# Transposed maxima on SP's queue, the projected values' rooms by turns, and another order for the first attention block

## The chip, the cores and the metric

The kernel runs on one core of a Trainium2 chip. The metric is the device time of one execution in microseconds, the median of several runs. The profiled execution has a time of its own, given below beside its span.

## The reference

Two attention blocks A and B are computed from inputs of their own, both with S = 2048 tokens, D = 512, H = 32 heads of 16 channels, in f32. A is a sliding window of 256 tokens, B sees all tokens.

```python
qkv = (x @ wqkv).reshape(B, S, 3, H, Dh)            # -> q, k, v: B, H, S, Dh
scores = einsum("bhqd,bhkd->bhqk", q, k) * Dh ** -0.5
# A only: mask = (i - j >= 0) & (i - j < 256), others to -1e9
p = softmax(scores, axis=-1)
o = einsum("bhqk,bhkd->bhqd", p, v)
out = o.transpose(...).reshape(B, S, D) @ wo
return concatenate([a, b], axis=-1)                 # 1, 2048, 1024
```

## The kernel before

**Precision.** PE's products are f32 or a split f32. An input is split into a rounded part and a rest (`split`, L137 on ACT and L138 on DVE or POOL), and a product of two split tiles is three matmuls (`products`, L183). One projection of 128 by 512 is so 4 x 3 = 12 matmuls.

**Projections.** There are 96 of them, 48 for each block, named in ORDER_P: `Aq20` is block A, queries, pair 2 of head groups, chunk 0 of 512 tokens, and `Av13` is block A, values, chunk 1, token tile 3 of that chunk. Queries and keys (`project_qk`) are evacuated by ACT (L241 or L245), split again on DVE (L251) or POOL (L255, L256), and stored to DRAM as `parts` (L263). From there they come back as `opk` (keys, `load_k_now`, L293) and `oq` (queries, `load_q_now`, L309), in a layout with 16 rows for each part of a head. Values (`project_v`) are evacuated by ACT into one of two SBUF rooms `vst` (L321) and stored as `vd` (L329); they return as `vt` (L337).

**Attention.** For each unit (block, head group of four heads, chunk of 512 queries) the largest score of each query is found first (`max_item`: matmuls at L416 for A and L368 for B, DVE at L421, L425, L426 or L372). `max_finish` negates the maxima and splits them in three bf16 parts, `max_rows` transposes them on PE (L464), ACT copies them to `ntr` (L466), and two transfers at L471 put them as three further rows under the queries in `oq`. With three rows of ones under the keys, the score matmul (`scores`, L497) so subtracts the maximum itself. ACT takes the exponential (L504), POOL masks A's tiles (L514), and `weigh` (L543, A) or `weigh2` (L528, B) multiplies with the values and a column of ones. The result goes to DRAM (`od`, L561), is normalised on POOL (L615 to L618), and projected by `wo`.

**Order.** All is scheduled by hand at build time. The block before B's attention runs by two strings. ORDER_A has a letter for each item on PE: `p` a whole projection (the next of ORDER_P), `m` a maximum, `t` a transposition of maxima, `s` a score step, `w` a weighing step, `e` an early maximum of B. The loop takes the letters strictly in turn. Products `p` and `t` use all rows of PE's array, `m`, `s` and `e` halves of it by rows, `w` quarters of it by columns. Around them a `Model` of the engines runs at build time; it decides where in the program the loads and the deferred work of the other engines are put: a load is written out when the model's time for PE has reached the time at which its data and room are there. Each engine then carries out its own instructions in the order written. The second block (B's attention) follows a fixed pattern and is not touched by ORDER_A.

**Transfers.** All are issued by SP, but for the rows of A's maxima (L471), which ACT issues. Each transfer signals one of eight semaphores, given out in turn over both queues, so that a transfer waits at its issue for the one eight places earlier to have landed. The model before has no such semaphores, and counts A's rows at L471 as ACT's time.

Of the kernel before, what the change touches and what calls it, by code (L numbers as in the profile page):

```python
# [11 lines left out]
F32 = mybir.dt.float32  # L12
# [18 lines left out]
KS = 3 * DH  # L31
KM = KS + 3
ROW = 0, 64
# [11 lines left out]


ORDER_P = (
# [4 lines left out]
    "Bq20 Bk13 Bk31 Bk30 Bq10 Bq30 Bk33 Bq31 Bq33 Bq32 Bk21 Bk32 ").split()  # L52
FIRST = 4.0
FINAL = 34.5
LOADS = 4.0
# [3 lines left out]


ORDER_A = (
    "ppppppppppmmpmmpmmpmmpmmptmmpmmpmsmpmsmpmsmpsmmtpmmswsmpswmmsptwmmspsmwmsmpsmwsmmpmswsmpsmmwtsmptmms"
    "psmmpmswsmpmswmsmpmswsmmswsmmswtmsmpsmmwsmsmwsmmstwmsmpsmwsmtwmmspmmswsmmswsmpsmmswsmmwsmsmtmspmmwsm"
    "psmmwsmtwsmmpmsmtmswmswsmsmmswmspmswmmswmspmssmwtsmmpmswtmsmpsmwsmswmssmmwsmpmmpmmswsmmswtsmmpsmmwsm"
    "smwstmmwsmpmsmwswsmmpmssmwtmsmpmssmmtwsmmpmswmsmsmwmssmtwsmmsmwmsmswmspsmwsmmswtmsmpwsmmswsmmpmswsmm"
    "psmmswtmsmpmswmsmpmmswtmsmpsmwmsmpsmwtmmspmswsmpsmwsmpmswtsmmpsmwsmwmspmswsmwtmmspswmmspsmmpsmwtmsmp"
    "smwmsmpmsmwspmsmwsmtwsmmpsmmwsmpsmwmsmpmswmsmpsemtwsmpemtpmsmwsmpmswemspsemswsempsempmswmmspmsmwsmtw"
    "mmspsempsmmwwtmsmpesmpmswsmmpsemswsmmswtmsmpmswmsmpesmwsmwmswemspsempemswwemtpesmpsmmwsmpemspmmswsmp"
    "mmtpsmmpmmwwm")
LAND = 700  # L70
LAND_V = 2000
LGAP = 2500
# [4 lines left out]
class Model:  # L77
# [4 lines left out]
    def __init__(self):  # L82
        self.t = {e: 0 for e in ("PE", "ACT", "DVE", "Pool", "SP", "DMA")}
        self.mode, self.turn = "f", 170
        self.banks = {"e": [0] * 3, "p": [0] * 2, "o": [0]}

    def run(self, engine, ns, *after):
        self.t[engine] = max(self.t[engine], *after, 0) + ns
# [6 lines left out]
        return self.run("PE", turn + ns, *after)  # L95

    def dma(self, kb, *after):
        t = self.run("SP", 450, *after) + 600
        self.t["DMA"] = max(self.t["DMA"], t) + int(4.0 * kb)
        return self.t["DMA"] + 1300  # L100

    def bank(self, pool, n=0):

# [15 lines left out]
def attention_kernel(ctx: ExitStack, tc: tile.TileContext, xT, wqk, wv, wo, out):  # L119

    nc = tc.nc
# [7 lines left out]
    M = Model()  # L129
    ready = {}  # L130
    obank = [None]
    ns = 0
    xs, ws, parts, vd, opq, mt, pts, pvt, od, rl, osp = {}, {}, {}, {}, {}, {}, {}, {}, {}, {}, {}
# [74 lines left out]
    vst = [cst.tile([128, H, VW], F32, name=f"vst{i}") for i in range(2)]  # L208
# [72 lines left out]
    def load_ones(g):  # L281
        for a in range(2):
            nc.sync.dma_start(opk2(g)[ROW[a] + KS:ROW[a] + KM].bitcast(F32), one_d.rearrange("(s r) t -> s r t", s=3))
            ready["ones", g % 2] = M.dma(48, ready["ones"])

    def load_k_now(b, g, c0, c1, t):

        ops = opk2(g)
        for a in range(2):
            for r, n in ((0, 2), (2, 1)):  # L290
                for c in range(c0, c1):
                    tok = slice(c * QC, c * QC + QC)
                    nc.sync.dma_start(ops[ROW[a] + 16 * r:ROW[a] + 16 * (r + n), :, tok].bitcast(F32),  # L293
                                      heads_of(b, g, 1, a)[0:n, :, :, tok])
                    t1 = M.dma(64 * n, t)
        for c in range(c0, c1):
            ready["k", b, g, c] = t1

# [4 lines left out]
    def load_q_now(b, g, c, t):  # L303

        oq = sb.tile([128, HG // 2, QC], F32R, name=f"oq_{b}_{g}_{c}", tag="oq", bufs=4)
        opq[b, g, c] = oq
        for a in range(2):
            for r, n in ((0, 1), (1, 2)):
                nc.sync.dma_start(oq[ROW[a] + 16 * r:ROW[a] + 16 * (r + n)].bitcast(F32),  # L309
                                  heads_of(b, g, 0, a)[0:n, :, :, c * QC:(c + 1) * QC])  # L310
                t1 = M.dma(64 * n, t)
        ready["qd", b, g, c] = t1

    def project_v(b, c, a):

        kt = 4 * c + a
        bank, ps = room()
        yield from products(ps, [(lambda u, i=i: xs[b, c, i][:, u, 128 * a:128 * a + 128], lambda v, i=i: ws[b, "v", i][:, v])
                      for i in range(4)])
        v = vst[kt % 2]  # L320
        nc.scalar.activation(v[:, :, 0:DH], ps.rearrange("p (h d) -> p h d", d=DH), AF.Copy)  # L321
        t = M.run("ACT", 480, M.t["PE"] + WAKE)
        release(bank, t)
        ready["vd", b, kt] = M.dma(272, t)
        slots_v.pop(0)
        slots_v.append(ready["vd", b, kt])
        if b not in vd:
            vd[b] = dram.tile([NG // 2, S, VP], F32, name=f"vd_{b}")
        nc.sync.dma_start(vd[b][:, kt * 128:kt * 128 + 128].rearrange("p t n -> t p n"),  # L329
                          v.rearrange("p (g h) d -> p g (h d)", g=NG // 2))  # L330
# [5 lines left out]
    def load_v_now(b, p, k0, k1, t):  # L336
        nc.sync.dma_start(vt[p % 2][:, k0:k1, 0:VP],  # L337
                          vd[b][p, k0 * 128:k1 * 128].rearrange("(k t) n -> t k n", t=128))
        t = M.dma(68 * (k1 - k0), t)
        for kt in range(k0, k1):  # L340
            ready["v", b, p, kt] = t

# [46 lines left out]
    def load_early_k(c):  # L389
        gap[0] = M.t["PE"] + GAP  # L390
        for a in range(2):
            for r, n in ((0, 2), (2, 1)):
                nc.sync.dma_start(ke()[ROW[a] + 16 * r:ROW[a] + 16 * (r + n), c * QC:c * QC + QC].bitcast(F32),
                                  heads_of(1, 0, 1, a)[0:n, :, 0, c * QC:c * QC + QC])
                ready["ke", c] = M.dma(32 * n)

    def max_item(b, g, c, qt, j, kc):
        n = f"{b}_{g}_{c}_{qt}_{j}_{kc}"
# [60 lines left out]
    def max_rows(b, g, c):  # L459
        n = f"{b}_{g}_{c}"  # L460
        nm = parts["nm"]
        bank, ps = room()
        ps = ps.bitcast(BF16)
        nc.tensor.transpose(ps[:48, :128], nm.rearrange("p a s j q -> p (a s j q)"), ident)  # L464
        nt = sb.tile([48, 128], F32, name=f"ntr_{n}", tag="ntr")
        nc.scalar.activation(nt, ps[:48, :128], AF.Copy)  # L466
        t = M.run("ACT", 200, M.pe("f", 60, ready["nm", b, g, c]))
        release(bank, t)
        for a in range(2):
            ready["q", b, g, c] = M.dma(12, t) if b else M.run("ACT", 775) + 2300  # L470
            (nc.sync if b else nc.scalar).dma_start(opq[b, g, c][ROW[a] + KS:ROW[a] + KM].bitcast(F32).rearrange(  # L471
                "s r (q t) -> s (r q) t", t=128), nt[24 * a:24 * a + 24])


# [280 lines left out]
    def pair(b, p):  # L755
        return [(project_qk, b, p, 1 - s, c) for c in range(NQC) for s in range(2)]

    def values(b):
        return [(project_v, b, c, a) for c in range(NQC) for a in range(4)]
# [16 lines left out]
    got = lambda its: all(x in made for x in its)  # L776
# [25 lines left out]
    def later_load(it, cond, f, *a):  # L802

        u = place.get(it, 0) - LOADS
        def g(*a):
            lgap[0] = M.t["PE"] + LGAP
            f(*a)
        list_("load", lambda: pos() >= u and cond(), lambda: max(lgap[0], free("stage")()), g, *a)
# [4 lines left out]
    for b, p in groups:  # L813
        its = values(b) if p == "v" else [] if p == "o" else pair(b, p)
        for s in range(4 if p in ("v", "o") else 2):
            before = slots_of[len(slots_of) - 8] if len(slots_of) >= 8 else []
            slots_of.append(its)
            cond = lambda before=before: got(before)
            it = its[0] if its else bursts[-1][1]
            later_load(it, cond, *((load_wv, b, s) if p == "v" else (load_wo, b, s) if p == "o" else  # L820
                                   (load_wqk, b, p, 1 - s)))
        if (b, p) == (1, 0):
            for c in range(NQC):
                for i in range(4):
                    later_load(pair(1, 0)[2 * c], lambda c=c: got(pair(0, 3)[0:2 * c + 2]), load_x, 1, c, i)

    def stored(b, p, s, cs):
        return lambda: max(ready.get(("parts", b, p, s, c), NEVER) for c in cs)
# [57 lines left out]
    while todo_a or gen[0]:  # L886
# [8 lines left out]
        i, j = divmod(ns, HG)  # L895
        t = NEVER
        if gen[0]:
            t = pe
        elif x == "p":
            t = max(bank(), operands(bursts[nb][1]))  # L900
        elif x == "t" and nts:
            t = max(ready["nm", *nts[0]], bank())
        elif x == "w" and k < i:
            un, (m, pieces), a, z = flat[k]
            t = max(*(ready.get(("v", 0, un[1] // 2, y[0]), NEVER) for y in pieces), ready["p", *un, m],
                    M.bank("o") if a else 0)
# [178 lines left out]
```

## Time and profile before

| | |
|---|---|
| median of 3 runs | 1906.01 us (1904.59 to 1915.66) |
| profiled execution | 1913.99 us, span 1912.3 us, granted clock 0.982 |
| PE busy | 1858.8 us (97%) |
| DVE busy | 1540.0 us (81%) |
| ACT busy | 1407.3 us (74%) |
| POOL busy | 469.2 us (25%) |
| instructions | 37273 |
| transferred | 166.68 MB |

Times in the profile count from the start of the span. PE is TensorE, PEld its weight loads, DVE VectorE, ACT ScalarE, POOL GpSimd, SP SyncE; a `q` behind an engine's name is its sequencer, which issues transfers. `L497` is line 497 of the program. A group of instructions is written as line, engine, operation, output<-inputs. A row of waits names who waited, for whom, how long in total, how many times, and the longest. Matmuls overlap, and their ends are modelled.

### The profile page before, as it was taken

Reading aid. Unit: us, or ns where it says so; the run is one execution under the profiler, and the core shown is the slowest. Engines: PE = TensorE matmul, PEld = TensorE weight load, DVE = VectorE, ACT = ScalarE, POOL = GpSimd, SP = SyncE. Lnnn points to the kernel's source line nnn. Section 1 sums busy time; section 2 is a strip of 40 time slices with the busy share of each in tenths; the row PEclk is TensorE's granted clock in tenths of the full one; section 3 lists DMA queues with packets and bytes.
Section 4 is the critical chain, followed back from the end, with each engine's and each line's share of the span. In section 5 each row is a group of like instructions: output and inputs, shape, how many; then the busy total and the mean of one; then the engine's idle time right before and its main releaser. Section 6 shows DMA issues by size and latency. Waiting matters only on the chain.

```text
span 1912.3 us, 37273 instructions
## 1 busy us (share of the span) xinstructions
PE 1858.8 (97%) x14376; PEld 935.9 (49%) x14376; DVE 1540.0 (81%) x2320; ACT 1407.3 (74%) x2754; POOL 469.2 (25%) x896
## 2 busy tenths in 40 slices
PE   7999898899999999999999999999999999999999
PEld 6665565566655455544444444444444444444436
DVE  4557578556657967699999999999999999999910
ACT  4256566555545867688888888888888888898883
POOL 0167677635564422001100000010001000001010
PEclk9999899899988999999999999999999999999999
DMA  7655565555445223411120031120031121010002
GB/s 246 178 176 166 162 181 174 172 140 161 152 142 166 82 82 90 97 41 33 28 74 15 15 72 33 44 63 16 29 71 28 32 61 35 16 37 21 30 30 94
DMA packets 129137, 166.68 MB, mean 87 GB/s; under 512 B 22996, under 2 KB 58836, under 8 KB 128948
## 3 DMA queue, kind: packets, MB, share of 16 engines
q1 hardware_dynamic: 127232, 163.52, 30.2%
q8 instruction: 113, 1.85, 0.4%
q10 hardware_dynamic: 1728, 0.79, 0.2%
q14 instruction: 64, 0.52, 0.1%
HBM read 94.49 MB, written 68.19 MB: 85 GB/s over the span
## 4 chain that ended last, share of the span: by engine, by line
PE 89%; DMA 4%; DVE 3%; ACT 2%; issue 1%; SPq 1%; ACTq 0%; POOL 0%
PE ps_all L528 28%; PE ps_all L368 19%; PE ps_all L497 18%; PE ps_all L183 17%; PE ps_all L543 4%; PE ps_all L416 2%; DVE mt L372 2%; ACT p L504 1%; DMA vd<-vst 1%; DMA in<-xT_A 1%; DMA opk<-parts 1%; PE ps_all L464 1%; DMA in<-xT_B 0%; DMA oq<-ntr 0%; DVE mt L426 0%
## 5 line engine op out<-in xcount | busy, mean ns | idle before, releaser
L504 ACT ACTIVATE p<-ps_all 128x512 f32<-128x512 f32 x2432 | 1261.6, 600 | 203.0 <-PE ps_all L497 117.7
L372 DVE TENSOR_REDUCE mt<-ps_all 128x2 f32<-128x1024 f32 x1516 | 1202.9, 869 | 89.5 <-PE ps_all L497 50.2
L497 PE MATMUL ps_all<-oq,opk 51*128 51x512 f32 (+2 forms) x2752 | 786.3, 413 | 13.9 <-ACT p L504 11.4
L368 PE MATMUL ps_all<-opk,oq 48*128 48x512 f32 x2016 | 679.2, 440 | 1.3 <-DVE mt L372 1.1
L528 PE MATMUL ps_all<-p,vt 128*32 128x256 f32 (+1 forms) x6056 | 601.5, 469 | 0.6 <-ACT ou L554 0.5
L497 PEld LDWEIGHTS ps_all<-oq,opk 51*128 51x128 f32 x2752 | 398.8, 187 | 221.1 <-ACT p L504 195.3
L368 PEld LDWEIGHTS ps_all<-opk,oq 48*128 48x128 f32 x2016 | 313.7, 185 | 321.9 <-DVE mt L372 146.5
L449 POOL TENSOR_SCALAR mm<-mm 128x16 f32<-128x16 f32 x31 | 7.8, 253 | 985.2 <-PE ps_all L497 843.3
L514 POOL TENSOR_SCALAR_AFFINE_SELECT p<-p 128x256 f32<-128x256 f32 x480 | 180.3, 407 | 234.2 <-ACT p L504 165.1
L528 PEld LDWEIGHTS ps_all<-p,vt 128*32 128x32 f32 x6056 | 119.8, 108 | 221.3 <-issue 210.6
L183 PE MATMUL ps_all<-x,w 128*128 128x512 f32 x768 | 202.5, 415 | 9.1 <-ACT w L137 9.1
L425 DVE COPY_PREDICATED ps_all<-mone,ps_all 128x256 f32<-128x256 uint16 x224 | 94.9, 424 | 119.6 <-PE ps_all L416 119.2
L183 PEld LDWEIGHTS ps_all<-x,w 128*128 128x128 f32 x768 | 146.7, 198 | 50.9 <-ACT w L137 9.3
L426 DVE TENSOR_REDUCE mt<-ps_all 128x2 f32<-128x512 f32 x224 | 155.3, 693 | 7.7
L183 PE MATMUL ps_all<-w_v,x 128*128 128x512 f32 x384 | 100.0, 412 | 5.8 <-ACT vst L321 4.4
L416 PE MATMUL ps_all<-opk,oq 48*128 48x384 f32 (+2 forms) x512 | 91.6, 378 | 11.2 <-DMA oq<-parts 9.1
L245 ACT ACTIVATE raw<-ps_all 128x512 f32<-128x512 f32 x56 | 33.4, 597 | 90.4 <-PE ps_all L183 88.1
L543 PE MATMUL ps_all<-p,vt 128*32 128x384 f32 (+2 forms) x1408 | 99.4, 398 | 0.0
L183 PE MATMUL ps_all<-w_o,x_o 128*128 128x512 f32 x384 | 90.4, 393 | 0.0
L183 PEld LDWEIGHTS ps_all<-w_v,x 128*128 128x128 f32 x384 | 72.7, 195 | 26.7 <-ACT vst L321 5.5
L183 PEld LDWEIGHTS ps_all<-w_o,x_o 128*128 128x128 f32 x384 | 71.2, 188 | 23.7 <-issue 6.7
L256 POOL TENSOR_TENSOR st<-raw,st 128x512 fp32r<-128x512 f32 x56 | 72.0, 1285 | 4.7
(58 smaller groups left out, 579.8 us busy)
## 6 DMA issues: line engine op xcount, KB each, us to landing
parts<-st SPq DMA_DIRECT2D x64, 512.0 KB
oq<-parts SPq DMA_DIRECT2D x128, 128.0 KB
opk<-parts SPq DMA_DIRECT2D x128, 128.0 KB
od<-ou SPq DMA_DIRECT2D x64, 256.0 KB
vd<-vst SPq DMA_DIRECT2D x32, 272.0 KB
oq<-parts SPq DMA_DIRECT2D x128, 64.0 KB
opk<-parts SPq DMA_DIRECT2D x128, 64.0 KB
t<-od SPq DMA_DIRECT2D x32, 256.0 KB
```

The lines of the kernel that those rows point to most:

```text
L183: nc.tensor.matmul(ps, l(u), r(v), start=start and k == 0, stop=stop and k == n - 1)
L256: nc.gpsimd.tensor_sub(two[:, 1], raw, two[:, 0].bitcast(F32))
L368: nc.tensor.matmul(ps[:, n], q[rows, 128 * qt:128 * qt + 128], k[rows, kc * QC:kc * QC + QC], start=True, stop=True)
L372: nc.vector.tensor_reduce(out=m[:, a:a + len(heads), r, qt, kc], in_=ps, axis=AX.X, op=ALU.max)
L416: nc.tensor.matmul(two[:, a, 0:w], opq[b, g, c][rows, r, 128 * qt:128 * qt + 128], opk2(g)[rows, r, t0:t1], start=True, stop=True)
L425: nc.vector.copy_predicated(two[:, :, 256:384], later, two[:, :, 0:128])
L426: nc.vector.tensor_reduce(out=m[:, :, r, qt, 0], in_=two[:, :, 128:384], axis=AX.X, op=ALU.max)
L497: nc.tensor.matmul(ps[x][:, col:col + n1], opk2(g)[rows, pr, 128 * k:128 * k + 128], opq[b, g, c][rows, pr, q0:q0 + n1], start=True, stop= ...
L504: nc.scalar.activation(p[:, a0 + x, :w], ps[x][:, :w], AF.Exp, scale=SCALE)
L514: nc.gpsimd.affine_select(out=v, in_=v, pattern=[[0, 2], [sign, 128]], compare_op=ALU.is_ge, fill=zero_fill, base=base, channel_multiplier ...
L528: nc.tensor.matmul(o[32 * j:32 * j + 32, q0:q1], vt[(g // 2) % 2][:, kt, vc:vc + 32], pts[1, g, c, kt, j // 2][:, j % 2, q0:q1], start=kt ...
L543: nc.tensor.matmul(o[32 * j:32 * j + 32, q0:q0 + w], vt[(g // 2) % 2][:, kt, vc:vc + 32], pts[b, g, c, m, j // 2][:, j % 2, col:col + w], ...
```

## The change

1. In `max_rows` the two transfers of A's rows are issued by SP, as B's already are, and no more by ACT.
2. In `project_v` the room is `vst[0]`, and the list is reversed after each use, so that the two rooms are used by turns in whatever order the values come. Before, the tile number's parity chose the room.
3. The model gives each transfer one of eight places (`lanes`) and makes SP wait for the place eight transfers back; it counts the rows of A as SP's; loads of `k`, `q`, `v` and the early ones can't start before the model's time of PE; the ones' rows are costed as 300 KB instead of 48.
4. The load of a chunk of B's input waits until all of A's projections that read the chunk before it in the same tiles are written out, not only those of pair 3.
5. ORDER_P and ORDER_A are searched anew on that model. They hold the same items in another order: 96 projections, and in ORDER_A 280 `m`, 192 `s`, 96 `p`, 96 `w`, 33 `t` and 16 `e` before and after.

```diff
 ORDER_P = (
-    "Aq00 Ak01 Ak00 Av13 Av01 Av00 Aq01 Ak02 Av22 Av03 Ak03 Aq02 Av23 Av10 Av31 Aq03 Av02 Av20 Av12 Av30 Av11 "
-    "Av21 Aq13 Ak10 Aq10 Ak20 Ak12 Av33 Ak11 Av32 Aq11 Aq12 Aq20 Ak30 Ak13 Aq31 Aq30 Aq23 Ak31 Aq22 Ak32 Bk00 "
-    "Aq21 Ak21 Ak23 Aq32 Ak22 Bq00 Aq33 Ak33 Bq02 Bk01 Bq01 Bk02 Bq03 Bk03 Bv32 Bv13 Bv00 Bv33 Bv23 Bv30 Bv11 "
...
+    "Aq00 Aq01 Ak00 Av11 Av13 Av20 Ak01 Av03 Aq02 Av01 Av22 Ak02 Av02 Av10 Aq03 Av30 Av21 Ak03 Av00 Av33 Av32 "
+    "Av12 Ak10 Aq10 Av23 Aq11 Ak20 Ak12 Av31 Aq22 Ak22 Aq13 Ak11 Aq12 Ak30 Ak13 Ak32 Ak31 Ak21 Aq30 Ak33 Aq31 "
+    "Aq20 Aq32 Aq21 Aq33 Aq23 Bk00 Ak23 Bq00 Bk01 Bk02 Bk03 Bq02 Bq03 Bq01 Bv13 Bv00 Bv02 Bv33 Bv30 Bv21 Bv32 "
...
 ORDER_A = (
-    "ppppppppppmmpmmpmmpmmpmmptmmpmmpmsmpmsmpmsmpsmmtpmmswsmpswmmsptwmmspsmwmsmpsmwsmmpmswsmpsmmwtsmptmms"
...
+    "pppppppppppmmpmmpmmpmmpmmtppmmspmmpmsmpmmspsmmtpmsmwsmsmpmsmwsmtwmspmmspmswsmmpsmwmsmpmmtpsmwsmmpmsw"
...
@@ class Model
         self.banks = {"e": [0] * 3, "p": [0] * 2, "o": [0]}
+        self.lanes = [0] * 8
...
     def dma(self, kb, *after):
-        t = self.run("SP", 450, *after) + 600
+        t = self.run("SP", 450, *after, self.lanes[0]) + 600
         self.t["DMA"] = max(self.t["DMA"], t) + int(4.0 * kb)
-        return self.t["DMA"] + 1300
+        self.lanes = [*self.lanes[1:], self.t["DMA"] + 1300]
+        return self.lanes[-1]
@@ load_ones
-            ready["ones", g % 2] = M.dma(48, ready["ones"])
+            ready["ones", g % 2] = M.dma(300, ready["ones"])
@@ load_k_now; the same for load_q_now, load_v_now, load_early_k
-                    t1 = M.dma(64 * n, t)
+                    t1 = M.dma(64 * n, t, M.t["PE"])
@@ project_v
-        v = vst[kt % 2]
+        v = vst[0]
+        vst.reverse()
@@ max_rows
-            ready["q", b, g, c] = M.dma(12, t) if b else M.run("ACT", 775) + 2300
-            (nc.sync if b else nc.scalar).dma_start(opq[b, g, c][...], nt[24 * a:24 * a + 24])
+            ready["q", b, g, c] = M.dma(12, t)
+            nc.sync.dma_start(opq[b, g, c][...], nt[24 * a:24 * a + 24])
@@ the loads of B's input
-                    later_load(pair(1, 0)[2 * c], lambda c=c: got(pair(0, 3)[0:2 * c + 2]), load_x, 1, c, i)
+                    later_load(pair(1, 0)[2 * c], lambda c=c: got([y for p in range(4) for y in pair(0, p)[0:2 * c + 2]] +
+                                                                  values(0)[0:4 * c + 4]), load_x, 1, c, i)
```

More of the change, by code (lines that the diff above doesn't have):

```diff
@@ L47 @@
 ORDER_P = (
[4 rows of a table removed]
-    "Bq20 Bk13 Bk31 Bk30 Bq10 Bq30 Bk33 Bq31 Bq33 Bq32 Bk21 Bk32 ").split()
[4 rows of a table added]
+    "Bk30 Bk31 Bq21 Bq13 Bq32 Bq23 Bk33 Bk32 Bq31 Bq33 Bk22 Bq30 ").split()
 FIRST = 4.0
@@ L61 @@
 ORDER_A = (
-    "ppppppppppmmpmmpmmpmmpmmptmmpmmpmsmpmsmpmsmpsmmtpmmswsmpswmmsptwmmspsmwmsmpsmwsmmpmswsmpsmmwtsmptmms"
[L63 to L69, printed above, removed]
+    "pppppppppppmmpmmpmmpmmpmmtppmmspmmpmsmpmmspsmmtpmsmwsmsmpmsmwsmtwmspmmspmswsmmpsmwmsmpmmtpsmwsmmpmsw"
+    "tmmspmsmwsmmswmspsmmwsmpmsmwtswmsmpmswtsmmswmspmsmswmsmpsmwtmmspsmwsmmswspmswsmpmsmwtsmmswsmpsmmwsmp"
+    "smwtsmmswsmmswsmmswmsptpwmsmswmsmswmsmsmswmsmpmwtmsmpmsmwsmmssmwmmtpmssmmwsmpsmmmwswmsmwmtpmmssmspms"
+    "mmwmswmtmswsmmsmpmmsmwtsmsmwmsmpmmssmtwsmpmsmwsmmswsmmswmsmsmptmmwsmsmwmspmmswsmpmswtmsmswmsmpmsmwts"
+    "mpsmmwsmpswmsmpsmmwsmpmsmwstwmsmpmswmmspmsmwtsmwsmmpsmwtsmmswsmpmswmsmpsmwmsmpmsmwtsmmswmspsmwtmmsps"
+    "mmswsmmswmspmswmmspmswtmsmpsmwsmmpmswsmmtpmsmwswmmspmswmsmpmswmsmptempmmswsmpemspmmswsmtwsempesmpesm"
+    "twsepemspmsmwsmwsempsmwsmmpsewsemsptempmsmwswmmspesmpmsmwsmwsmmpesmpsmmptewesmwsmwmsmpmsmpsempsmwsmm"
+    "psmmptmmwwwmm")
 LAND = 700
@@ L310, in load_q_now @@
                                   heads_of(b, g, 0, a)[0:n, :, :, c * QC:(c + 1) * QC])
-                t1 = M.dma(64 * n, t)
+                t1 = M.dma(64 * n, t, M.t["PE"])
         ready["qd", b, g, c] = t1
@@ L338, in load_v_now @@
                           vd[b][p, k0 * 128:k1 * 128].rearrange("(k t) n -> t k n", t=128))
-        t = M.dma(68 * (k1 - k0), t)
+        t = M.dma(68 * (k1 - k0), t, M.t["PE"])
         for kt in range(k0, k1):
@@ L394, in load_early_k @@
                                   heads_of(1, 0, 1, a)[0:n, :, 0, c * QC:c * QC + QC])
-                ready["ke", c] = M.dma(32 * n)
+                ready["ke", c] = M.dma(32 * n, M.t["PE"])
     def max_item(b, g, c, qt, j, kc):
@@ L469, in max_rows @@
         for a in range(2):
-            ready["q", b, g, c] = M.dma(12, t) if b else M.run("ACT", 775) + 2300
-            (nc.sync if b else nc.scalar).dma_start(opq[b, g, c][ROW[a] + KS:ROW[a] + KM].bitcast(F32).rearrange(
+            ready["q", b, g, c] = M.dma(12, t)
+            nc.sync.dma_start(opq[b, g, c][ROW[a] + KS:ROW[a] + KM].bitcast(F32).rearrange(
                 "s r (q t) -> s (r q) t", t=128), nt[24 * a:24 * a + 24])
```

2 rows, old and new, of the table ORDER_P are left out of this document.

## The prediction, made before the changed kernel was run

> **What bounds the kernel now.** I read the page first, then busy time by stretches, the waits of PE and of ACT, and last the order of time around each long wait.
>
> ```profile
> span 1912.3 us, 37273 instructions
> ```
>
> ```profile
> 0.00:603.20 603.20, 555.97 (x3908) 367.93 (x3908) 376.56 (x800) 311.19 (x615) 332.99 (x644) 0.96 0.58 172
> 603.20:1912.30 1309.10, 1302.82 (x10469) 567.98 (x10468) 1163.46 (x1521) 1096.15 (x2140) 136.24 (x252) 0.99 0.19 48
> ```
>
> ```profile
> L528 PE MATMUL ps_all<-p,vt x6056: 379/403/1061, 603.2 to 1875.2; 128*32 128x256 f32 x126, 128*32 128x512 f32 x70
> ```
>
> The columns of a stretch are PE, PEld, DVE, ACT and POOL busy, the granted clock, and DMA. L528 belongs to the second attention block alone, so the first block ends at 603.2. Behind it PE has 6.3 us of idle time in 1309; the change leaves that stage's order alone, and I put it at 0. Ahead of it PE has 603.20 - 555.97 = 47.2 us of idle time. There DVE, ACT and POOL are each under two thirds busy, so PE waits for single late events and not for a slow engine. The waits of PE in that stretch (total, times, longest):
>
> ```profile
> PE ps_all L497 <- ACT p L504: 10.9, 19, 4.4
> PE ps_all L183 <- ACT w L137: 9.1, 1, 9.1
> PE ps_all L416 <- DMA oq<-parts: 9.1, 3, 7.1
> PE ps_all L464 <- ACT raw L245: 5.2, 1, 5.2
> PE ps_all L183 <- ACT vst L321: 4.4, 1, 4.4
> PE ps_all L464 <- ACT vst L321: 2.6, 1, 2.6
> ```
>
> The 9.1 us at L183 are the first load and stay. Five of the others are single stops of 2.6 to 7.1 us, and they cost twice, because the granted clock is halved around them:
>
> ```profile
> 73.30:80.10 6.80, 5.57 (x14) 3.96 (x14) 0.00 (x0) 1.58 (x3) 1.12 (x3) 0.50 0.86 237
> 189.30:192.70 3.40, 3.40 (x11) 2.54 (x10) 2.00 (x8) 1.60 (x3) 2.16 (x5) 0.51 0.63 222
> 209.80:226.90 17.10, 14.25 (x75) 8.53 (x75) 7.42 (x16) 9.00 (x19) 10.21 (x20) 0.50 0.87 244
> 336.10:346.30 10.20, 6.33 (x16) 4.58 (x16) 1.20 (x8) 2.23 (x4) 3.65 (x5) 0.50 0.80 198
> 397.60:401.00 3.40, 3.40 (x10) 2.62 (x9) 1.68 (x3) 1.08 (x2) 1.12 (x3) 0.50 0.48 130
> 537.50:547.70 10.20, 8.33 (x30) 5.75 (x31) 2.36 (x2) 5.26 (x10) 6.92 (x11) 0.50 0.51 163
> 602.40:612.60 10.20, 10.20 (x53) 3.34 (x50) 7.09 (x10) 5.63 (x11) 0.00 (x0) 0.50 0.94 158
> ```
>
> What PE loses there is read from one and the same burst of 12 products, slow and fast, in the chain:
>
> ```profile
> 189.56 4.47 PE ps_all L183 x12
> ...
> 196.24 2.95 PE ps_all L183 x12
> ```
>
> (4.47 - 2.95) / 4.47 = 0.34 of the busy time at half clock. What ACT did ahead of the stops, in the order of time (the bracket is its idle time and what ended it):
>
> ```profile
> 73.88 0.60 ACT L321 ACTIVATE vst<-ps_all 128x512 f32<-128x512 f32 x1 [6.64 <-DMA vd<-vst]
> 208.50 0.63 ACT L137 ACTIVATE x<-in 128x512 fp32r<-128x512 f32 x1 [3.08 <-DMA in<-xT_B]
> 211.26 0.63 ACT L137 ACTIVATE x<-in 128x512 fp32r<-128x512 f32 x1 [2.13 <-DMA in<-xT_B]
> 338.16 0.63 ACT L137 ACTIVATE x<-in 128x512 fp32r<-128x512 f32 x1 [5.94 <-DMA in<-xT_B]
> 395.13 0.60 ACT L321 ACTIVATE vst<-ps_all 128x512 f32<-128x512 f32 x1 [5.13 <-DMA vd<-vst]
> 538.20 0.63 ACT L137 ACTIVATE w<-in 128x512 fp32r<-128x512 f32 x1 [7.11 <-DMA in<-wqk_B]
> ```
>
> So ACT, which works in order, stood still for a transfer while PE's banks waited for it. Two stops have the room `vst` as their cause, the others loads that went out or landed late.
>
> **The change part by part.** *The rooms.* Before, the parity of the token tile picks the room, and in the old ORDER_P 14 of the 31 steps from one value to the next keep the parity, so that the evacuation waits for the store just issued:
>
> ```profile
> ACT vst L321 <- DMA vd<-vst: 23.0, 6, 6.6
> ```
>
> Taking turns leaves none of these 14 (the new order would have 13 by parity). The 4.4 and 2.6 us go, and with them the slow windows at 73.3 and 397.6: (5.57 + 3.40) x 0.34 = 3.0. Together **10.0 us**. Next late would be the store before the last; a product lies between, 2.95 us, so what remains of a 5 to 6 us wait is 2 to 4 us at the worst, and the order around it is new anyway. I take nothing for it.
>
> *The transposed maxima.* In the first block 64 transfers leave ACT for SP:
>
> ```profile
> L471 ACTq DMA_DIRECT2D oq<-ntr x64: 728/729/1327, 60.3 to 566.2; - x64
> L471 SPq DMA_DIRECT2D oq<-ntr x64: 712/746/855, 588.1 to 1828.5; - x64
> ```
>
> ACT is rid of 64 x 0.729 = 46.7 us of issuing; with 311 of 603 us busy it has the idle time to hide that now, so it counts nothing by itself. At most it shortens the small waits for `p`, 10.9 - 4.4 = 6.5 us; I take 0 and keep 6.5 for the low end. SP gains 64 x 0.746 = 47.7 us. SP is covered too:
>
> ```profile
> SPq L561 <- ACT ou L554: 60.2, 17, 6.0
> SPq L329 <- ACT vst L321: 48.1, 18, 7.5
> SPq L293 <- DMA oq<-ntr: 21.3, 7, 9.2
> ...
> SPq L309 <- DMA oq<-ntr: 12.2, 4, 6.1
> SPq L151 <- DMA oq<-ntr: 12.2, 2, 7.8
> ```
>
> It waits 108 us of the block for two kinds of tiles that ACT writes. The last three rows are the point of the change: 45.7 us in which SP could not issue a load because ACT had not yet issued, or not landed, an earlier transfer with the same one of eight semaphores. Such a wait sent the load late on which ACT stands at 208.50:
>
> ```profile
> 202.52 1.49 ACTq L471 DMA_DIRECT2D oq<-ntr  x2
> ```
>
> ```profile
> 204.74 0.36 SPq L151 DMA_DIRECT2D in<-xT_B  x1
> ```
>
> The load went out 2.2 us behind the row transfers, as soon as the first of them had landed. In the new program SP itself waits at L471 for the rows. Queued behind it are the loads of keys and queries (L293, L309), of inputs (L151) and the stores (L263, L329, L561), and who waits for these is PE at L416 and ACT at L137 and L321.
>
> *The order anew*, on a model that now has the eight semaphores and SP's share of L471. PE's items are the same in number. In ORDER_A the changes between products, half-height and column tiles fall from 386 to 376:
>
> ```profile
> PEld ps_all L543 <- issue: 22.7, 109, 0.4
> ```
>
> 22.7 / 109 = 0.21 us each, **2.1 us** for ten. The stops that are not those of the rooms: 9.1 (L416) + 5.2 (L464) + 4.4 (L497) = 18.7 us, and the slow windows at 189.3, 209.8, 336.1 and 537.5, (3.40 + 14.25 + 6.33 + 8.33) x 0.34 = 11.0; together 29.7. Between nothing (or new stops, below) and all of it, I take half, **14.9 us**: their cause, a transfer held by one eight places back, is what the new model counts, but landing times that it does not know (one wait of 7.11, another of 2.13 us for the same kind of load) will make others. The window at 602.4 belongs to no stop over 1.1 us and stays.
>
> *The guard on the second block's inputs* (all readers of a chunk) costs nothing: in the new ORDER_P the last reader of chunk 0 is place 42 and the first product with the new chunk place 47. A place is 603.2 / 96 = 6.3 us of the block, so 31 us cover the load and split; without the cover it is a stop like that of 5.2 us. The model's other new terms (PE's time as the earliest for a load, 300 KB for the ones) issue no instruction; they only shift where the program puts loads, which is in the half above.
>
> The trace's granted clock drops at 397.6 behind 2.6 us of idle time, and at 189.3 behind none that its waits show as long. The Trainium skill ("TensorE: Matmul & The Clock Gate", "Why this matters for your kernels") gives idle gaps of over some 3 us as the cause of a drop; by that the window at 397.6 would stay, and the sum be 1.2 us less. The trace does not bear the limit out.
>
> **Sum**: 10.0 + 14.9 + 2.1 = 27.0 us against the profiled execution, whose 1912.3 us of span with 1.7 around it are 1913.99. That is 8.0 over the median of 1906.01 (1904.59 to 1915.66), so a median run probably lacks part of these stops. Of 10.0 + 29.7 = 39.7 us it can lack 8.0; I scale by 31.7 / 39.7 = 0.8: 21.6 us, and 1906.0 - 21.6 = **1884**.
>
> **The rivals.** *Only the rooms help.* The new order meets as many held transfers as the old. For it: 10.9 us in 19 waits show how many near misses there are; against it: 45.7 us of one kind of wait have their cause removed. (10.0 + 2.1) x 0.8 = 9.7, so **1896**. The Trainium skill ("DMA: Bandwidth & Descriptors", "Issuing engines are not separate DMA queues") says that choosing another issuing engine only moves the sequencer's issue time; by that rule the move from ACT to SP is worth nothing, which is this rival. The 45.7 us of SP's waits speak against the "only": a semaphore held by the other queue is more than issue time.
>
> *SP is held by the rows, slower.* Before, SP often passes the place of a row transfer long ahead of it:
>
> ```profile
> 520.27 3.79 SPq L293 DMA_DIRECT2D opk<-parts  x6
> ```
>
> ```profile
> 531.12 1.50 ACTq L471 DMA_DIRECT2D oq<-ntr  x2
> ```
>
> Six key loads went out 7 to 11 us before the row transfers that, by the turn of the semaphores, stand directly ahead of them; in the new program they follow. It decides once the load behind a held row is needed by PE sooner than the hold is long. If one in four of the 32 pairs becomes a stop like the six of now (the 9.1 us counted as two), (7.0 + 18.7) / 6 + 41.3 x 0.34 / 6 = 6.6 us, that is 53 us: 1906 - 21.6 + 53 = **1937**. For it: the loads of queries were late by 7.1 us once already. Against it: the stores behind ACT hold SP to PE's pace in any case, 108 us.
>
> *The stops only move.* New ones make up for all that goes: **1906**.
>
> **How the numbers follow.** Forecast 0.53 (1867 to 1895), rooms only 0.22, moved 0.12, held 0.13. About 1% (19 us) is what a measurement can tell here. Of the forecast's chance 0.44 lies below 1887; 0.09 with the second and third case makes 0.43 within; 0.13 slower. Low end: all 39.7, with 2.1 and 6.5, is 48.3 x 0.8 = 38.6, so 1867, rounded to 1866. High end: 1906 with half of the runs' spread of 11 us, 1912. Outside lie the last case and tails.
>
> **What the changed profile would show.** L528 starts near 577 and the stage behind it still takes about 1309. L471 is on SP alone, x128. ACT's 23.0 us for `vd<-vst` fall under 6. No wait of SP names a row transfer's landing for more than 10 us in all; waits at L471 for ACT's `ntr` appear. PE's idle time ahead of L528 is 28 to 33 us, and fewer slow windows lie there. I am wrong if PE's L416 or L497 wait for `opk`, `oq` or rows in more stops than now, if ACT still stands at L137 for 5 us, or if slow windows stay where no stop is.

## The result and the profile after

The changed kernel takes 1879.62 us (median of 4 runs, 1874.48 to 1883.77) against 1907.04 us (4 runs), a ratio of 0.9847 with a 95% interval of 0.9802 to 0.9892. The forecast was 1884. The sum came out; the experiments show that two of its terms stood in the wrong place.

The page's span, after (the second transfer queue, ACT's, is not on the page any more):

```profile
span 1872.8 us, 37299 instructions
```

The first block ends where B's weighing begins, which is line 532 after the change. The row of that line, then busy time by stretches (PE, PEld, DVE, ACT, POOL, granted clock, DMA):

```profile
L532 PE MATMUL ps_all<-p,vt x6056: 378/403/1062, 569.6 to 1835.7; 128*32 128x256 f32 x126, 128*32 128x512 f32 x70
```

```profile
0.00:569.60 569.60, 541.77 (x3908) 359.33 (x3908) 384.85 (x800) 312.85 (x615) 332.39 (x644) 0.99 0.60 181
569.60:1872.80 1303.20, 1297.08 (x10469) 567.39 (x10468) 1162.74 (x1521) 1095.65 (x2140) 136.35 (x252) 1.00 0.19 49
234.30:237.70 3.40, 3.40 (x9) 2.21 (x7) 0.46 (x1) 0.34 (x1) 2.45 (x2) 0.51 0.30 100
285.50:288.90 3.40, 3.40 (x23) 1.66 (x23) 1.82 (x4) 1.51 (x5) 3.31 (x7) 0.51 0.48 125
302.60:306.00 3.40, 3.40 (x10) 2.72 (x9) 1.62 (x3) 1.08 (x3) 3.40 (x8) 0.50 0.85 252
565.40:572.20 6.80, 6.80 (x29) 3.72 (x27) 5.54 (x8) 4.20 (x8) 0.00 (x0) 0.50 0.45 137
```

The two profiled executions are 39.5 us of span apart, more than the medians, because that of before was a long one and that of after a short one. 33.6 us of it lie in the first block. PE's idle time there falls from 47.2 to 569.60 - 541.77 = 27.8 us, 19.4 less. The stretches at half clock that begin ahead of the second block fall from seven with 61.3 us to four with 17.0.

What such a stretch costs is more than the prediction's 0.34 of the busy time. Its slow burst ran from 189.56 to 194.03, beyond the end of the half-clock stretch at 192.70. The chain of before has another burst of the same 12 products that lies wholly inside a stretch, that from 73.30 to 80.10:

```profile
74.53 5.49 PE ps_all L183 x12
```

(5.49 - 2.95) / 5.49 = 0.46. So the first six stretches of before lost 19.0 us, and the three of after and the part of the fourth ahead of 569.6 lose some 6.6. That is 12.4 us less, with 1.8 us left that I can't assign.

PE's waits and SP's in the first block, after:

```profile
PE ps_all L186 <- ACT w L140: 9.0, 1, 9.0
PE ps_all L420 <- DVE mt L430: 7.8, 15, 1.5
PE ps_all L501 <- ACT p L508: 5.3, 17, 0.5
PE ps_all L372 <- DVE mt L376: 1.9, 1, 1.9
```

```profile
SPq L333 <- ACT vst L325: 47.2, 19, 5.7
SPq L565 <- ACT ou L558: 39.5, 19, 4.4
SPq L475 <- ACT ntr L470: 38.1, 12, 6.8
```

Beside the first load no stop of PE is longer than 1.9 us; the five of 2.6 to 7.1 us are gone. In SP's waits there is no row with the landing of a row transfer, and SP now waits at L475 (L471 before) for ACT's `ntr`, as said beforehand. That wait stands in part where others stood: SP's for ACT's `ou` fell from 60.2 to 39.5 us.

### The profile page after: what moved, and what is told of

The parts are those of the page before. It is cut to its first block, busy times and chain, and to the rows that moved or that the text cites. A ratio compares the mean times of both kernels' runs of the same rounds, so it can differ in the third digit from the quotient of the medians.

```text
span 1872.8 us, 37299 instructions
## 1 busy us (share of the span) xinstructions
PE 1838.9 (98%) x14376; PEld 926.7 (49%) x14376; DVE 1547.6 (83%) x2320; ACT 1408.5 (75%) x2754; POOL 468.7 (25%) x896
## 4 chain that ended last, share of the span: by engine, by line
PE 91%; DVE 5%; DMA 1%; ACT 1%; issue 1%; SPq 1%; POOL 0%; ACTq 0%; POOLq 0%
PE ps_all L532 29%; PE ps_all L372 19%; PE ps_all L186 18%; PE ps_all L501 18%; PE ps_all L547 4%; PE ps_all L420 3%; DVE mt L376 2%; DVE mt L430 1%; DVE ps_all L429 1%; ACT p L508 1%; PE ps_all L468 1%; DMA vt<-vd 1%; DVE nm L460 0%; DMA in<-xT_A 0%; DVE nr L458 0%
## 5 line engine op out<-in xcount | busy, mean ns | idle before, releaser
L186 PE MATMUL ps_all<-x,w 128*128 128x512 f32 x768 | 197.6, 407 | 9.0 <-ACT w L140 9.0
L186 PEld LDWEIGHTS ps_all<-x,w 128*128 128x128 f32 x768 | 142.9, 192 | 49.4 <-ACT w L140 9.0
L420 PE MATMUL ps_all<-opk,oq 48*128 48x384 f32 (+2 forms) x512 | 91.8, 377 | 9.1 <-DVE mt L430 7.8
L547 PE MATMUL ps_all<-p,vt 128*32 128x384 f32 (+2 forms) x1408 | 98.6, 393 | 0.3 <-POOL p L518 0.3
L186 PE MATMUL ps_all<-w_v,x 128*128 128x512 f32 x384 | 95.1, 398 | 0.2 <-ACT p L508 0.2
L186 PEld LDWEIGHTS ps_all<-w_o,x_o 128*128 128x128 f32 x384 | 71.2, 188 | 23.7 <-issue 8.4
```

Of the source, the lines that this page charges most:

```text
L186: nc.tensor.matmul(ps, l(u), r(v), start=start and k == 0, stop=stop and k == n - 1)
L420: nc.tensor.matmul(two[:, a, 0:w], opq[b, g, c][rows, r, 128 * qt:128 * qt + 128], opk2(g)[rows, r, t0:t1], start=True, stop=True)
L547: nc.tensor.matmul(o[32 * j:32 * j + 32, q0:q0 + w], vt[(g // 2) % 2][:, kt, vc:vc + 32], pts[b, g, c, m, j // 2][:, j % 2, col:col + w], ...
```

## The experiments

Each was timed against the kernel before on the same chip; the ratio is to that kernel. "Rows" are the transposed maxima of block A.

**1. The rooms alone.** The kernel before with

```diff
-        v = vst[kt % 2]
+        v = vst[0]
+        vst.reverse()
```

> The kernel before with only the two rooms for projected values used by turns; order, model and issuing engines as before. If the stops behind the rooms are worth what the prediction's sum says (10.0 us, scaled 8), the time is about 1899 us, ACT's wait for vd<-vst falls from 23.0 to under 6 us, and the stops of 4.4 us at 74.5 and 2.6 us at 395.8 are gone with their slow windows. If the old order just stops at the next late transfer instead, it is within 3 us of 1907.

Measured: 1904.55 us, 0.9963 [0.9949, 0.9977], or 7 us of 1912. ACT's wait and PE's waits in the first block:

```profile
ACT vst L322 <- DMA vd<-vst: 9.5, 3, 4.0
```

```profile
PE ps_all L498 <- ACT p L505: 11.4, 19, 4.4
PE ps_all L417 <- DMA oq<-parts: 10.2, 5, 6.2
PE ps_all L183 <- ACT w L137: 9.6, 1, 9.6
PE ps_all L465 <- ACT raw L245: 5.4, 1, 5.4
...
PE ps_all L183 <- ACT vst L322: 1.2, 1, 1.2
```

The 4.4 us at L183 became 1.2, and the 2.6 us at L464 became 0.4; ACT's wait fell from 23.0 to 9.5 and not under 6, because three values still come sooner than the store before the last lands. The stops for late loads (4.4, 6.2, 5.4 us) stay much as they were (4.4, 7.1, 5.2).

**2. The queue alone.** The kernel before with

```diff
-            (nc.sync if b else nc.scalar).dma_start(...)
+            nc.sync.dma_start(...)
```

> The kernel before with only the rows of A's maxima issued by SP; order, model and rooms as before. If the queue itself is what costs (semaphores held by ACT's transfers, 45.7 us of SP's waits), the time falls by about 12 us to 1895. If only the order, made with SP's share in mind, makes use of it, the time stays within 4 us of 1907. If SP is held by the rows, the prediction's slower rival, it is 10 to 50 us longer and PE's waits at L416 for oq or opk grow.

Measured: 1884.99 us, 0.9865 [0.9851, 0.9879]: 26 us from one line, in an order that was not made for it. PE's waits in the first block:

```profile
PE ps_all L183 <- ACT w L137: 10.3, 1, 10.3
PE ps_all L497 <- ACT p L504: 5.7, 16, 0.5
PE ps_all L416 <- DVE mt L426: 4.6, 8, 1.8
PE ps_all L183 <- ACT vst L321: 3.7, 1, 3.7
PE ps_all L464 <- ACT vst L321: 2.4, 1, 2.4
```

All stops for late loads are gone (`oq<-parts` of 7.1 and two short ones of 2.0 together, `raw` of 5.2, `p` of 4.4), and the two stops behind the rooms are left, the reverse of the first experiment. SP's waits that have to do with the rows:

```profile
SPq L561 <- ACT ntr L466: 20.7, 5, 5.5
SPq L471 <- ACT ntr L466: 13.8, 6, 5.3
```

There is no wait for a row's landing. The prediction's slower rival, SP held by the rows, falls: the holds are there, and no stop of PE for `oq` or `opk` comes of them.

**3. Both edits, old order, old model.**

> The kernel before with both edits, rooms by turns and rows on SP, but the old order and the old model. If the two edits carry the gain, about 1887 us or less. If the order carries it, 1899 (the rooms alone). If SP is held by the rows with an order that does not know of it, over 1907.

Measured: 1878.91 us, 0.9831 [0.9817, 0.9845]. This is as fast as the whole change. The edits add up: 0.0037 and 0.0135 make 0.0172, and 0.0169 is what came.

**4. All but the order strings.** The changed kernel with the old ORDER_P and ORDER_A.

> The changed kernel with the two old order strings: the new model, which places the loads, both edits and the guard are in, only the order of PE's items is the old one. If the placing of loads by the better model does the work, about 1885. If the order strings carry it, 1895 to 1910, with single stops of 3 to 7 us left in the first block.

Measured: 1887.05 us, 0.9860 [0.9838, 0.9881]. That is near the 1885 expected if the placing of the loads did the work, but the third experiment has no less of a gain without the new model. So its placing of the loads brings nothing over that; if anything it costs a few us.

**5. The new order with the rows on ACT again.** The changed kernel with the second experiment's line turned back.

> The changed kernel with only the rows of A's maxima back on ACT's queue; new order, new model, rooms by turns. If the queue carries gain, about 1892 (12 us more than 1880), with SP again waiting some 40 us for row transfers. If the order carries it, within 4 us of 1880 although these waits come back.

Measured: 1936.18 us, 1.0130 [1.0107, 1.0153]. Neither expectation was near: the queue is worth 54 us in this order ((1.0130 - 0.9847) x 1912), twice that of the old one. SP's waits and PE's in the first block:

```profile
SPq L296 <- DMA oq<-ntr: 34.3, 7, 9.6
...
SPq L312 <- DMA oq<-ntr: 18.0, 4, 7.6
SPq L579 <- DMA oq<-ntr: 13.7, 2, 8.0
SPq L333 <- DMA oq<-ntr: 9.1, 2, 8.8
SPq L565 <- DMA oq<-ntr: 8.8, 2, 7.7
```

```profile
PE ps_all L501 <- ACT p L508: 18.4, 27, 1.8
...
PE ps_all L420 <- DMA oq<-parts: 8.0, 3, 4.8
PE ps_all L547 <- POOL p L518: 6.1, 1, 6.1
```

The waits for rows are 83.9 us; before, all waits of this kind were about 53 us, 45.7 of them in the three rows shown there. And the small waits for `p` are more than three times those of the change (5.3 us). One of them in the order of time, on ACT and on PE:

```profile
208.95 1.50 ACTq L475 DMA_DIRECT2D oq<-ntr  x2
210.55 1.64 ACT L508 ACTIVATE p<-ps_all 128x384 f32<-128x384 f32 x4 [1.63 <-POOL st L258]
```

```profile
211.09 0.44 PE L501 MATMUL ps_all<-oq,opk 51*128 51x384 f32 x1 [1.58 <-ACT p L508]
```

ACT is idle for 1.63 us because it issues for 1.50, and PE waits for 1.58 of them. The releaser in ACT's bracket (POOL) is not the cause; the sequencer's own work is.

**6. The new order with the room by parity.** The changed kernel with the first experiment's lines turned back.

> The changed kernel with the room chosen by the tile's parity again (13 of 31 steps keep it). By the prediction's sum for the rooms about 8 us more than 1880, 1888, with ACT's wait for vd<-vst back at some 20 us and one or two stops of 3 to 4 us on PE. If the new order leaves enough time between values, within 3 us of 1880.

Measured: 1880.21 us, 0.9836 [0.9812, 0.9859], no different from the change. ACT waits 16.3 us for `vd<-vst` in four places, and PE waits for `vst` 0.8 us in two: here the values have room enough around them.

**7. and 8. The order without its edits.** First both edits undone in the changed kernel, then nothing but the two strings in the kernel before.

> The changed kernel with both edits undone, rows on ACT and rooms by parity; new order, model and guard stay. If the edits carry the gain, about 1900. If the order and the model that places the loads carry it, 1880 to 1888 (the rooms' part at most).

> The kernel before with nothing but the two new order strings; the old model, which places the loads, the queue, the rooms and the guard as before. If the strings carry the gain by themselves, 1880 to 1888, like the run with both edits undone. If they need loads placed by the model that they were searched on, the time is longer than that, 1895 or more, with stops at L416 or L497 for loads.

Measured: 1932.71 us, 1.0105 [1.0082, 1.0127], and 1929.72 us, 1.0095 [1.0074, 1.0116]. The first is far from both of its figures. The strings by themselves make the kernel before 1% slower. That is over the 1895 expected if they need loads placed by their model, but not for that reason: with the model, in the first of the two runs, the time is the same (the intervals overlap).

**9. Six stops made on purpose.** The changed kernel with, for six units,

```diff
         nt = sb.tile([48, 128], F32, ...)
+        if b == 0 and c == 1 and g >= 2:
+            for _ in range(26):
+                nc.scalar.activation(idle_out, wmask[:, 0:128], AF.Copy)
```

> The changed kernel with 26 further ACT copies of 128x128 (about 0.27 us each, 7 us in one go) ahead of the copy of the rows of six units (chunk 1 of six head groups in A), which change no output. Before, ACT's standstills of 5 to 7 us gave PE stops of 2.6 to 4.4 us, that is the standstill less some 2.4. If a stop costs twice, as the prediction has it, the six give 6 x 4.6 = 28 us of idle time on PE and some 14 us more through windows at half clock: 1880 + 42 = 1922. If the halved clock is no consequence of stops, 1880 + 28 = 1908 without new slow windows. If PE has slack for them, under 1890.

Measured: 1939.61 us, 1.0129 [1.0105, 1.0154], which is 54 us more than the change. The copies stood 0.34 us apart and held ACT 8.8 us, not 7. PE's waits, and the stretches at half clock:

```profile
PE ps_all L505 <- ACT ntr L474: 26.8, 4, 8.0
PE ps_all L186 <- ACT ntr L474: 15.8, 2, 8.1
```

```profile
194.60:215.10 20.50, 15.45 (x78) 9.28 (x79) 6.53 (x15) 11.28 (x31) 5.36 (x14) 0.50 0.53 151
273.10:283.30 10.20, 6.70 (x18) 4.78 (x19) 2.73 (x7) 6.14 (x18) 6.20 (x9) 0.50 0.50 136
337.90:348.10 10.20, 6.05 (x29) 3.64 (x30) 2.50 (x5) 7.14 (x21) 2.56 (x6) 0.50 0.25 71
402.80:413.00 10.20, 5.13 (x14) 3.83 (x15) 3.40 (x8) 7.28 (x22) 3.16 (x6) 0.50 0.20 61
464.20:474.40 10.20, 3.74 (x9) 2.97 (x10) 0.39 (x2) 6.79 (x22) 1.13 (x3) 0.50 0.14 39
532.50:542.70 10.20, 4.29 (x10) 3.42 (x11) 0.00 (x0) 6.79 (x21) 0.76 (x2) 0.50 0.19 69
```

Each of the six has its slow stretch. 42.6 us of idle time and 41.4 x 0.46 = 19.0 us at half clock make 61.6. The times show 54, by their intervals some 10 more or less; in the two traces the first blocks are 633.9 - 569.6 = 64.3 us apart. So a stop of some 7 us costs its length and a little under a half more.

**10. and 11. ACT's time without its semaphores.** The second experiment, and the changed kernel, each with

```diff
+        if b == 0:
+            for _ in range(5):
+                nc.scalar.activation(idle_out, wmask[:, 0:128], AF.Copy)
```

behind the copy of the rows.

> The second experiment (old order, rows on SP) with five further ACT copies of 128x128 behind the copy of the rows of each of A's 32 units, 0.34 us apart or 1.7 us together: the time that issuing the two transfers took on ACT (1.5 us), without its semaphores. They change no output. If the gain of the move came from the semaphores that SP no longer shares with ACT, it stays within 5 us of 1885. If it came from ACT's time, it goes back to 1905 to 1912. In between, it is both.

> The changed kernel with the same five ACT copies behind the copy of the rows of each of A's 32 units. The same change of queue was worth 56 us in the new order (1936 against 1880). If the semaphores made that, the time stays within 5 us of 1880. If ACT's 1.5 us did, at which PE stopped again and again for p (1.3 to 1.8 us), it is 1925 to 1936. In between, it is both, and the difference shows the shares.

Measured: 1882.27 us, 0.9834 [0.9814, 0.9853] in the old order, and 1898.43 us, 0.9924 [0.9908, 0.9940] in the new one. In the old order ACT's time is worth nothing. What is left for the 26 us of the second experiment are the shared semaphores, and the trace of the kernel before shows them at work ahead of each long stop for a late load (PE goes on at 212.43, 339.63 and 539.37). SP's waits for a row's landing just before these, from 196 to 206, from 312 to 334 and from 519 to 535:

```profile
SPq L151 <- DMA oq<-ntr: 7.8, 1, 7.8
```

```profile
SPq L293 <- DMA oq<-ntr: 7.8, 2, 6.2
```

```profile
SPq L293 <- DMA oq<-ntr: 9.2, 1, 9.2
```

The records of the transfers name the semaphore that each signals. ACT's row of 202.52 and the load that SP then issued at 204.74 have the same one, number 109; so have the row of 325.36 and the load of 327.57 (107), and the row of 531.12 and the load of 533.33 (109). The input and weight loads at which ACT stood (208.50, 338.16 and 538.20) were the first of these loads or queued behind them. Not tried is ACT's queue with semaphores of its own; the next experiment has another queue with its own.

In the new order ACT's time makes (0.9924 - 0.9847) x 1912 = 15 us of the 54, and PE's waits show how:

```profile
PE ps_all L505 <- ACT p L512: 15.6, 26, 1.6
```

against 5.3 us in 17 waits. The other 39 us, by subtraction, are then the semaphores'; as the change's own interval is 0.009 or 17 us wide, the split is rough. One reserve: in both kernels SP's transfers went out only behind the copies, so the rows were up to 1.7 us late as well, and in the new order SP waited 67.8 us for the copies, where in the change it waits 38.1 us for `ntr`. Beside the first load PE has no wait for a row or a load over 0.3 us that this could explain, but ACT's share is rather an upper end.

**12. The rows on POOL.** The first experiment with the rows issued by POOL.

> The kernel before with the rooms by turns and the rows of A's maxima issued by POOL, so that neither ACT nor SP issues them and SP isn't held by them. If it is only leaving ACT and its shared semaphores that counts, about 1879 as with SP; if SP's waits at L471 cost something too, some us less. If POOL's own work on these transfers, and its standing still for the rows, delay the masks (L514) that the weighing waits for, over 1890.

Measured: 1893.27 us, 0.9899 [0.9881, 0.9918]: 13 us slower than with SP. By the records, POOL's transfers signal eight semaphores of their own (111 to 118) and share none with SP. SP has no wait for a row's landing, and beside the first load PE has no stop for a late one (for rows it waits 2.3 us in four places): this second queue, which shares no semaphores, does not hold SP. The time is lost elsewhere. PE waits 8.1 us for DVE at L417, and 3.0 us at L465 for DVE's parts of the maxima, where the kernel with SP has 4.6 and 1.0; nothing waits for late masks. What came on DVE ahead of the longest of these, 2.9 us at L417, and POOL at that time:

```profile
262.68 3.39 DVE L457 TENSOR_TENSOR nm<-nr,nm 128x16 bf16<-128x16 f32 x1
```

```profile
262.01 1.15 POOL L472 DMA_DIRECT2D oq<-ntr  x2
263.17 0.42 POOL L515 TENSOR_SCALAR_AFFINE_SELECT p<-p 128x256 f32<-128x256 f32 x1
263.54 2.49 POOL L138 TENSOR_TENSOR x<-in,x 128x512 fp32r<-128x512 f32 x2
```

The subtraction of 16 columns, 0.27 us on average before, took 3.39 us and ended when POOL's two operations on SBUF did. The four small operations that make a unit's parts (L454 to L457) take 53.4 us of DVE, 45.3 with SP. That this is why the kernel is slower than with SP was not tested by itself.

## Why the prediction was right, and where it was not

- *What bounds the kernel*: right. The gain came in the first block, from its single long stops and the half clock around them. The ninth experiment shows the double cost, 54 us for stops of 42.6. The factor of 0.34 was misread from a burst that was only in part at half clock; with 0.46 the prediction's 3.0 and 11.0 us become 4.1 and 14.9, and its sum 30.0 instead of 27.0.
- *The second stage at 0*: it became 5.9 us shorter. Two stretches at half clock, most of the one that before began at 602.4 and one at 1820.9, are what I see missing in it. It is no gain of the change: the same stage takes 1308.7 us in the sixth experiment and 1303.2 in the fifth, and 1303 to 1310 over all traces.
- *The rooms, 10.0 us (8 scaled)*: 7 us in the old order (experiments 1 and 3). In the new order they measure nothing (experiment 6). So the term holds for the kernel before, not for the change as a whole.
- *The transposed maxima, "it counts nothing by itself"*: this step failed. ACT's time is indeed nothing in the old order (experiment 10), but the semaphores, which the same part called the point of the change, were given no term. They measure 26 us there (experiments 2 and 10).
- *The order anew, 14.9 us and 2.1*: also failed. With the edits in place the new strings bring nothing that could be measured (0.9847 against 0.9831, with intervals of 9 and 3 us to either side), and without them they cost 1% (experiments 7 and 8). I had booked the late-load stops to the order; one line of the queue removes all of them. The half that I took of 29.7 us was too little for the queue and too much for the order, and the two errors cancelled; that the sum came out is luck in this part. The row from which the 2.1 us were read did not fall either: 22.7 us in 109 waits at L543 before, 23.7 in 117 at L547 after.
- *Rivals*: "only the rooms help" is refuted by the second experiment: 26 us came from leaving the second engine although the issue time on the first grew. With it falls, for this program, what the Trainium skill ("DMA: Bandwidth & Descriptors", "Issuing engines are not separate DMA queues") states, that starting transfers on several engines at once only saves the sequencer's time to start them. "SP is held" was refuted there too. "The stops only move" is refuted by the result.
- *What the profile would show*: the first block's end near 577 (569.6), idle time of 28 to 33 us (27.8, just under), `vd<-vst` under 6 us (no such row any more), no wait for a row's landing, waits at L475: all there or close. But one of its signs of being wrong came as well: slow stretches where no stop is, at 234.3, 285.5 and 302.6. What made them stays open. The order left a trace of its own that I had not named: 7.8 us of waits at L420 for DVE, 1.5 us before.

What stays open is why the new order's semaphores cost more with ACT's rows than the old one's (39 against 26 us). The 83.9 us of SP's waits say that they do, not which places make it.

## What to carry to other kernels

Where two queues draw in turn from one small set of completion semaphores, here eight, a transfer on one can have to wait for the transfer eight places back on the other, and so for that engine's backlog; look in the issuing queue's waits for landings that it did not issue itself. Read the cause of each long stop before pricing a reordering: here one line removed what a new search seemed to be needed for, and only undoing one part at a time told them apart. An order searched on a model is worth what it is only with the assumptions of that model; with the rows back on ACT the same strings lost 54 us.

## What the runs showed of the hardware

- Short stretches at half clock (3.4 us each) came also where PE had no stop over 1.5 us, at 234.3, 285.5 and 302.6 after the change.
- At half clock a burst of 12 products took 5.49 us, 2.95 at full.
- A DVE operation on 16 columns with two SBUF inputs took 3.39 us beside POOL's two-input operations. The Trainium skill ("SBUF — State Buffer", "SBUF: two separate sides") states that such a DVE operation and a POOL operation that reads SBUF share one port pair, which the one that starts first holds for its whole instruction while the other is blocked. The trace agrees in that the DVE operation ended at 266.07 and POOL's second one at 266.03; that DVE was held over two POOL operations in a row is more than the page states.
